# A one-token attention and FFN kernel: weight loads on 128 + 64 partitions, a split last V chunk, late softmax normalisation and a pre-gated FFN row

## The chip, the cores and the metric

The kernel runs on one core of a Trainium2 chip. The metric is device time in microseconds (us), best read as a median of several executions. A profile of one execution is looked at beside it; its span is about 1.8 us shorter than the time. Some numbers are taken from the trace's own records: of every DMA packet it has start, length and size, and of every load it has the sixteen moments at which the load's sixteen shares landed; I take one share for one of the sixteen DMA engines, which the records do not name. PE is the matrix engine, ACT and DVE are the two engines for element-wise work, and SP issues the loads. In this kernel PE's results go to the memory PSUM, and the loaded tensors lie in the memory SBUF on 128 partitions or fewer, each with its own rows. A granted clock of 1.00 is PE's full clock in the profile, 0.50 half of it.

## The reference

A single token `x` (448 values) goes through attention with 16 query heads over 8 cached K/V heads of 65536 keys (head size 256), and through a gated FFN. The two rows are mixed by a sigmoid gate.

```python
def reference(A_x, A_k_cache, A_v_cache, A_wq, A_wo, B_x, B_W_gate, B_W_up, B_W_down, gate_w):
    x = A_x                                            # [1, 1, 448], bf16
    g = sigmoid((x * gate_w).sum(-1, keepdims=True))
    q = (x @ A_wq) as 16 heads of 256
    p = softmax(q @ k.T * 256 ** -0.5)                 # k, v: [8, 65536, 256], each used by two heads
    a = (p @ v) as one row of 4096 @ A_wo
    b = (relu(x @ W_gate) * (x @ W_up)) @ W_down       # F = 1792
    return g * a + (1 - g) * b
```

K and V are 537 MB together. Every byte is used once, so this is a kernel that streams.

## The kernel before

One queue (the SP engine's) issues all loads in a fixed order into a ring of seven slots of 2 MB. A slot is reloaded when PE has consumed what lay in it. PE transposes K groups (ACT moves them from PSUM to SBUF), multiplies them with q, and later multiplies the transposed probabilities with V. The weights share one SBUF region, `wreg`.

The parts that the change touches (cuts marked):

```python
KC = 112                                   # 448 rows of weights = 112 partitions x 4 rows
wq_v = wreg[0:KC, 0:NKC * HQ * DH].rearrange("p (c n) -> p c n", c=NKC)
# ... W_gate and W_up likewise; W_down and A_wo are on 128 partitions

# SP: the stream of loads
sp.dma_start(xT[:, :], ...); sp.dma_start(gwT[:, :], ...)
sp.dma_start(wq_v, A_wq.rearrange("(p c) n -> p c n", c=NKC)).then_inc(s_wq, 16)
for i, (kind, p, c) in enumerate(stream):  # 256 chunks of 2 MB
    # ... wait until the slot is free
    sp.dma_start(ring[:, b], chunk_src(kind, p, c)).then_inc(s_arr[b], 16)
    # after chunk 3: W_gate, W_up, W_down; after chunk 18: A_wo

# PE: PV, 16 matmuls per chunk, in turn on three column tiles (NPV = 3) of one PSUM bank
ins = pe.matmul(ps[32 * ct:32 * ct + 4, PV, :], lhsT=pT_bf[...], rhs=ring[:, b, 2 * k:2 * k + 2, :], ...)

# DVE, at the end of each head: scale the three tiles one after the other
for ct in range(NPV):
    ins = dve.tensor_scalar(o8[32 * ct:32 * ct + 4, p % 2, :], ps[32 * ct:32 * ct + 4, PV, :],
                            rl[32 * ct:32 * ct + 4, p:p + 1], None, ALU.mult)
# PE: OT (sum of the tiles, transposed) -> DVE: copy to oT -> PE: N (times A_wo)
# DVE, at the very end: out = (N - b) * g + b
n = self_inc(dve.tensor_tensor(res_f[R, :], row_ps(), b_sb[R, :], ALU.subtract))
dve.scalar_tensor_tensor(res_b[R, :], res_f[R, :], e_sb[R, 2:3], b_sb[R, :], ALU.mult, ALU.add)
```

## Time and profile before

| What | Before |
|---|---|
| time, median of the 13 runs beside the change's | 1325.9 us |
| span of the profiled execution | 1322.7 us |
| bytes loaded | 549 MB |
| PE / ACT / DVE busy | 73% / 42% / 3% |
| last V chunk has landed | 1312.8 us |
| from there to the end | 9.9 us |

The page of the kernel before cuts the span into 40 slices. `PEclk` is the granted clock of PE in tenths, `DMA` the busy share of the 16 DMA engines in tenths, `GB/s` what they moved.

```profile
PEclk9799988979879988988889889888988889888866
DMA  9999999999999999999999999999999999999994
GB/s 316 336 427 418 420 427 428 428 428 427 427 427 428 428 426 427 428 427 426 428 427 427 427 428 427 427 427 427 428 427 427 427 428 425 429 428 427 428 428 197
```

The DMA engines are busy throughout, and 427 to 428 GB/s is their steady rate. The kernel is bound by its loads. Only the first two slices and the last fall short, so these are where time can be won. The stretch table gives, for each stretch of the kernel before, the busy time of PE, PEld (weight loading), DVE, ACT and POOL, then the granted clock, the DMA share and GB/s.

```profile
2.00:19.00 17.00, 0.20 (x8) 0.23 (x9) 1.43 (x6) 0.01 (x1) 0.00 (x0) 1.00 0.98 261
36.00:53.00 17.00, 8.29 (x82) 5.62 (x80) 0.00 (x0) 7.12 (x14) 0.00 (x0) 0.92 1.01 251
1300.00:1309.00 9.00, 3.75 (x31) 1.09 (x32) 0.00 (x0) 0.00 (x0) 0.00 (x0) 0.64 0.52 224
```

From 2 to 19 us `A_wq` loads, and from 36 to 53 us `W_gate` and `W_up`. The engines are fully busy (shares 0.98 and 1.01) and move 60% of their steady rate. At the end it is different: the busy share is one half, because eight of the sixteen shares have landed or nearly so. The first share of the last chunk landed at 1298.05 us, seven of them by 1299.8, the eighth at 1303.9 and the slowest at 1312.8.

The end of the chain of waits of the kernel before: start, duration, and what it was (engine, tile written, line).

```profile
1281.41 31.39 DMA ring<-in_A_v_cache_dram
1312.84 2.40 PE ps L422 x16
1315.26 0.74 DVE o L609
1316.03 0.75 DVE o L609
1316.81 0.76 DVE o L609
1318.13 1.67 PE ps L474 x4
1319.83 0.64 DVE res_f L636
1320.49 0.69 DVE res_b L638
```

After the last landing all is serial: 16 matmuls of the probabilities with V (PV, L422), three scalings (L609), the four matmuls with `A_wo` (L474), two final operations.

### The profile page before, as it was taken

The numbers are of one execution on the slowest core, as the hardware profiler recorded it, in microseconds if no ns is written. First come the engines' busy times: TensorE is split into PE (matmuls) and PEld (weight loads), VectorE is DVE, ScalarE is ACT, GpSimd is POOL, SyncE is SP. The second block draws the span as 40 slices with busy tenths as digits, with TensorE's granted clock in tenths as the row PEclk, the third lists the DMA queues.
The fourth block names the chain that finished last, engine by engine and source line by source line (L and its number), as shares of the span: only waits on it lengthen the run. The fifth ranks groups of instructions, "written<-read, shape, count | busy, mean of one in ns | idle before, by whom it ended". The sixth has DMA issues, their size and how long they took to land.

```text
span 1322.7 us, 18879 instructions
## 1 busy us (share of the span) xinstructions
PE 959.0 (73%) x8618; PEld 636.2 (48%) x8618; DVE 43.6 (3%) x113; ACT 556.4 (42%) x1066; POOL 0.6 (0%) x6
## 2 busy tenths in 40 slices
PE   3499876768777777777777687776977768767644
PEld 3377554545554455455544454453645445455211
DVE  0000000000000100001000010000100000000101
ACT  2368543435444444434434354442634435434100
POOL 0000000000000000000000000000000000000000
PEclk9799988979879988988889889888988889888866
DMA  9999999999999999999999999999999999999994
GB/s 316 336 427 418 420 427 428 428 428 427 427 427 428 428 426 427 428 427 426 428 427 427 427 428 427 427 427 427 428 427 427 427 428 425 429 428 427 428 428 197
DMA packets 43505, 550.25 MB, mean 416 GB/s; under 512 B 4433, under 2 KB 10322, under 8 KB 10322
## 3 DMA queue, kind: packets, MB, share of 16 engines
q1 hardware_dynamic: 43426, 549.05, 98.8%
q8 instruction: 68, 1.11, 0.3%
q14 instruction: 11, 0.09, 0.0%
HBM read 549.03 MB, written 0.00 MB: 415 GB/s over the span
## 4 chain that ended last, share of the span: by engine, by line
DMA 74%; PE 24%; ACT 1%; DVE 0%; issue 0%; SPq 0%
DMA ring<-in_A_k_cache_dram 64%; PE ps L376 16%; DMA ring<-in_A_v_cache_dram 9%; PE ps L395 4%; PE ps L422 3%; DMA wreg<-in_A_wq_dram 1%; ACT pb L515 1%; PE ps L356 0%; ACT ktb L525 0%; PE ps L493 0%; DVE o L609 0%; PE ps L437 0%; PE ps L474 0%; PE ps L433 0%; PE ps L483 0%
## 5 line engine op out<-in xcount | busy, mean ns | idle before, releaser
L525 ACT COPY ktb<-ps 128x512 f32<-128x512 f32 x1024 | 540.1, 598 | 644.4 <-PE ps L376 643.3
L376 PE MATMUL ps<-ident_f,ring 128*128 128x128 f32 x4096 | 594.4, 306 | 262.0 <-DMA ring<-in_A_k_cache_dram 256.8
L376 PEld LDWEIGHTS ps<-ident_f,ring 128*128 128x128 f32 x4096 | 518.7, 158 | 396.0 <-DMA ring<-in_A_k_cache_dram 307.7
L422 PE MATMUL ps<-ring,pT_all 128*4 128x512 bf16 x2048 | 207.3, 409 | 74.5 <-DMA ring<-in_A_v_cache_dram 72.6
L395 PE MATMUL ps<-ktb,zq 128*32 128x512 bf16 x2048 | 177.7, 424 | 0.0
L422 PEld LDWEIGHTS ps<-ring,pT_all 128*4 128x4 bf16 x2048 | 66.5, 87 | 193.5 <-DMA ring<-in_A_v_cache_dram 108.1
L395 PEld LDWEIGHTS ps<-ktb,zq 128*32 128x32 bf16 x2048 | 31.9, 96 | 49.9 <-ACT ktb L525 48.6
L577 DVE TENSOR_REDUCE mB<-ps 128x1 f32<-128x512 f32 x8 | 5.5, 691 | 649.4 <-PE ps L395 649.4
L609 DVE TENSOR_SCALAR o<-ps,rl 4x512 bf16<-4x512 f32 x24 | 17.8, 743 | 63.5 <-PE ps L422 63.0
L577 DVE TENSOR_REDUCE mA<-ps 128x1 f32<-128x512 f32 x8 | 5.5, 691 | 386.9 <-PE ps L395 386.9
L356 PE MATMUL ps<-xT,wreg 112*128 112x1 bf16 x128 | 3.6, 165 | 18.8 <-DMA wreg<-in_A_wq_dram 18.8
L515 ACT ACTIVATE pb<-ps,negM 128x512 bf16<-128x512 f32 x16 | 10.8, 682 | 7.2 <-DVE negM L593 7.2
L356 PEld LDWEIGHTS ps<-xT,wreg 112*128 112x128 bf16 x128 | 3.5, 104 | 18.8 <-issue 18.8
L474 PE MATMUL ps<-wreg,oT 128*1 128x448 bf16 x32 | 8.1, 379 | 2.0 <-DVE oT L617 2.0
L510 ACT ACTIVATE e_sb<-ps 1x1 f32<-1x1 f32 x1 | 0.2, 163 | 20.8 <-DVE zq L555 20.8
L530 ACT COPY pT_all<-ps 128x512 f32<-128x512 f32 x8 | 4.7, 586 | 9.4 <-PE ps L453 9.4
L453 PE MATMUL ps<-ident_b,pb 128*128 128x128 bf16 x64 | 5.2, 228 | 0.0
L453 PEld LDWEIGHTS ps<-ident_b,pb 128*128 128x128 bf16 x64 | 4.7, 114 | 0.0
L462 PEld LDWEIGHTS ps<-sel_b,o 128*128 128x128 bf16 x32 | 1.3, 98 | 6.9 <-issue 3.5
L442 PEld LDWEIGHTS ps<-rs,wpar_f 128*128 128x128 f32 x16 | 2.6, 203 | 4.0 <-issue 4.0
L437 PEld LDWEIGHTS ps<-ident_f,negR 1*128 1x128 f32 x16 | 2.3, 182 | 3.6 <-issue 3.6
L462 PE MATMUL ps<-sel_b,o 128*128 128x2 bf16 x32 | 2.0, 167 | 2.4 <-DVE o L609 2.4
(45 smaller groups left out, 43.4 us busy)
## 6 DMA issues: line engine op xcount, KB each, us to landing
ring<-in_A_k_cache_dram SPq DMA_DIRECT2D x128, 2048.0 KB, 31.5
ring<-in_A_v_cache_dram SPq DMA_DIRECT2D x128, 2048.0 KB, 29.6
wreg<-in_A_wq_dram SPq DMA_DIRECT2D x1, 3584.0 KB, 17.0
wreg<-in_A_wo_dram SPq DMA_DIRECT2D x1, 3584.0 KB, 31.5
wreg<-in_B_W_gate_dram SPq DMA_DIRECT2D x1, 1568.0 KB, 24.5
wreg<-in_B_W_up_dram SPq DMA_DIRECT2D x1, 1568.0 KB, 30.6
wreg<-in_B_W_down_dram SPq DMA_DIRECT2D x1, 1568.0 KB, 34.1
xT<-in_A_x_dram SPq DMA_DIRECT2D x1, 0.9 KB, 1.8
```

Source lines behind the costliest of these rows:

```text
L356: ins = pe.matmul(ps[:, PX, XC_Q + cq:XC_Q + cq + 1], lhsT=wq_v[:, ic, hq * DH + par:(hq + 1) * DH:2], rhs=xT[:, ic:ic + 1], start=(ic == ...
L376: ins = pe.transpose(ps[:, ts % 3, s * 128:(s + 1) * 128], ring[:, b, j, :].bitcast(F32), ident_f[:, :])
L395: ins = pe.matmul(ps[32 * c:32 * c + 32, bank, :], lhsT=zq[:, p, par, 30 - 2 * u:62 - 2 * u], rhs=kt_bf[:, par:1024:2], start=(u == 0 and ...
L422: ins = pe.matmul(ps[32 * ct:32 * ct + 4, PV, :], lhsT=pT_bf[:, p % 2, col0:col0 + 4], rhs=ring[:, b, 2 * k:2 * k + 2, :], start=(kk == ct ...
L453: ins = pe.transpose(dstv[:, o0:o0 + 128], pb[:, p % 2, bb, s * 128:(s + 1) * 128], ident_b[:, :])
L462: ins = pe.matmul(ps[:, PX, XO + hf * 2:XO + hf * 2 + 2], lhsT=o8[:, p % 2, sp_ * 256 + hf * 128:sp_ * 256 + (hf + 1) * 128], rhs=sel_b[:, ...
L474: ins = pe.matmul(row_ps(), lhsT=oT[:, cc:cc + 1], rhs=wo_sb[:, cc, :], start=(p == 0 and k == 0), stop=(p == HKV - 1 and k == 3), tile_po ...
L515: ins = act.activation(pb[:, p % 2, bb, :], ps[:, sbank(p, bb), :], AF.Exp, bias=negM[:, p:p + 1], scale=1.0, accum_out=rs[:, p, bb:bb + 1])
L525: act.copy(ktb[:, g % NKT, :], ps[:, ts % 3, :]).then_inc(s_ev, 1)
L530: act.copy(pT_all[:, p % 2, :].rearrange("k (bb r s) -> k bb r s", bb=2, r=GPB, s=4), ps[:, ts % 3, :].rearrange("k (bb s r) -> k bb r s", ...
L577: return self_inc(dve.tensor_reduce(dst[:, p:p + 1], ps[:, sbank(p, bb), :], AX.X, ALU.max))
L609: ins = dve.tensor_scalar(o8[32 * ct:32 * ct + 4, p % 2, :], ps[32 * ct:32 * ct + 4, PV, :], rl[32 * ct:32 * ct + 4, p:p + 1], None, ALU.mult)
```

## The change

Its name speaks of the decode tail, but it also changes how the weights are laid out. The core of the diff, with cuts:

```diff
-    KC = 112
-    NKC = D // KC
+    NKA = 3                                  # 384 rows on 128 partitions ...
+    KB = D - 128 * NKA                       # ... and 64 rows on 64 partitions
+    NKC = NKA + 1
-            sp.dma_start(wq_v, A_wq.rearrange("(p c) n -> p c n", c=NKC)).then_inc(s_wq, 16)
+            sp.dma_start(wqA, A_wq[0:128 * NKA, :].rearrange("(p c) n -> p c n", c=NKA)).then_inc(s_wq, 16)
+            sp.dma_start(wqB, A_wq[128 * NKA:D, :]).then_inc(s_wq, 16)
 ...  (W_gate, W_up, x and gate_w are split in the same way)
+    TAIL=((0, 16), (16, 8), (24, 8)),        # the last V chunk as three loads
 ...
+        def npv_of(p):                       # two column tiles in the last head
+            return 2 if (p == HKV - 1 and NPV > 2) else NPV
 ...
-                    ins = dve.tensor_scalar(o8[...], ps[32 * ct:32 * ct + 4, PV, :], rl[...], None, ALU.mult)
+                    ins = dve.tensor_copy(o8[...], ps[32 * ct:32 * ct + 4, PV, :])   # last head: tile 0
+                act.copy(o8[32:36, (HKV - 1) % 2, :], ps[32:36, PV, :])              # last head: tile 1
 ...
-                dve.tensor_copy(oT[...], ps[:, PX, XO:XO + 4]...)
+                dve.tensor_tensor(oT[...], ps[:, PX, XO:XO + 4]..., rlq[...], ALU.mult)   # 1/sum here
 ...
-                dve.tensor_copy(b_sb[R, :], row_ps())
+                dve.tensor_scalar(gb_sb[R, :], row_ps(), e_sb[R, 3:4], None, ALU.mult)    # (1-g)*b, early
-            n = self_inc(dve.tensor_tensor(res_f[R, :], row_ps(), b_sb[R, :], ALU.subtract))
-            dve.scalar_tensor_tensor(res_b[R, :], res_f[R, :], e_sb[R, 2:3], b_sb[R, :], ALU.mult, ALU.add)
+            dve.scalar_tensor_tensor(res_b[R, :], row_ps(), e_sb[R, 2:3], gb_sb[R, :], ALU.mult, ALU.add)
```

The intent: loads without odd partition counts at the start, and after the last byte 4 matmuls instead of 16, one PSUM copy time instead of three, one final operation instead of two.

More of the change, by code (lines that the diff above doesn't have):

```diff
@@ L39, in bass_gated_mix__gqa_block_cached__glu_gated_reglu__decode_kernel @@
     assert DH == 256 and HQ == 2 * HKV
-    KC = 112
-    NKC = D // KC
-    assert NKC * KC == D
+    NKA = 3
+    KB = D - 128 * NKA
+    assert 0 < KB <= 128
+    NKC = NKA + 1
     FC = 128
@@ L76, in bass_gated_mix__gqa_block_cached__glu_gated_reglu__decode_kernel, with geom @@
             vi += 1
-    for c in range(CPH):
+    for c in range(CPH - 1):
         stream.append(("V", HKV - 1, c))
+    sub = {}
+    for (j0, n) in TAIL:
+        item = ("V", HKV - 1, CPH - 1 + len(sub))
+        sub[item] = (CPH - 1, j0, n)
+        stream.append(item)
+    assert sum(n for (_, n) in TAIL) == CS and all(n % 2 == 0 and j0 % 2 == 0 for (j0, n) in TAIL)
     NCHUNK = len(stream)
+    def geom(item):
+        if item in sub:
+            return sub[item]
+        return (item[2], 0, CS)
     def gidx(p, c, gi):
@@ L190, in bass_gated_mix__gqa_block_cached__glu_gated_reglu__decode_kernel @@
         ring = es.enter_context(nc.sbuf_tensor("ring", [128, NB, CS, DH], BF))
-        wreg = es.enter_context(nc.sbuf_tensor("wreg", [128, NKC * F * 2 + NFC * D], BF))
+        WREG = max(NKC * HQ * DH, 2 * NKC * F + NFC * D)
+        wreg = es.enter_context(nc.sbuf_tensor("wreg", [128, WREG], BF))
         ktb = es.enter_context(nc.sbuf_tensor("ktb", [128, NKT, 512], F32))
@@ L202, in bass_gated_mix__gqa_block_cached__glu_gated_reglu__decode_kernel @@
         sel_f = es.enter_context(nc.sbuf_tensor("sel_f", [128, 32], F32))
-        sel_b = es.enter_context(nc.sbuf_tensor("sel_b", [128, 4], BF))
-        xT = es.enter_context(nc.sbuf_tensor("xT", [KC, NKC], BF))
-        gwT = es.enter_context(nc.sbuf_tensor("gwT", [KC, NKC], BF))
+        sel_b = es.enter_context(nc.sbuf_tensor("sel_b", [128, 2, 4], BF))
+        ones_f = es.enter_context(nc.sbuf_tensor("ones_f", [128, 128], F32))
+        rsq = es.enter_context(nc.sbuf_tensor("rsq", [128, HKV, 2], F32))
+        gb_sb = es.enter_context(nc.sbuf_tensor("gb_sb", [RP + 1, D], F32))
+        xT = es.enter_context(nc.sbuf_tensor("xT", [128, NKC], BF))
+        gwT = es.enter_context(nc.sbuf_tensor("gwT", [128, NKC], BF))
         oT = es.enter_context(nc.sbuf_tensor("oT", [128, NQC], BF))
@@ L215, in bass_gated_mix__gqa_block_cached__glu_gated_reglu__decode_kernel @@
         rs2 = es.enter_context(nc.sbuf_tensor("rs2", [128, HKV], F32))
-        rl = es.enter_context(nc.sbuf_tensor("rl", [128, HKV], F32))
+        rlq = es.enter_context(nc.sbuf_tensor("rlq", [128, HKV, 2], F32))
         r_sb = es.enter_context(nc.sbuf_tensor("r_sb", [128, NFC], F32))
         hT = es.enter_context(nc.sbuf_tensor("hT", [128, NFC], BF))
-        b_sb = es.enter_context(nc.sbuf_tensor("b_sb", [RP + 1, D], F32))
         e_sb = es.enter_context(nc.sbuf_tensor("e_sb", [RP + 1, 4], F32))
-        res_f = es.enter_context(nc.sbuf_tensor("res_f", [RP + 1, D], F32))
         res_b = es.enter_context(nc.sbuf_tensor("res_b", [RP + 1, D], BF))
@@ L243, in bass_gated_mix__gqa_block_cached__glu_gated_reglu__decode_kernel, with wsplit, wparts @@
         pT_bf = pT_all[:, :, :].bitcast(BF)
-        wq_v = wreg[0:KC, 0:NKC * HQ * DH].rearrange("p (c n) -> p c n", c=NKC)
-        wg_v = wreg[0:KC, 0:NKC * F].rearrange("p (c n) -> p c n", c=NKC)
-        wu_v = wreg[0:KC, NKC * F:2 * NKC * F].rearrange("p (c n) -> p c n", c=NKC)
+        def wsplit(off, n):
+            a = wreg[:, off:off + NKA * n].rearrange("p (c n) -> p c n", c=NKA)
+            b = wreg[0:KB, off + NKA * n:off + NKC * n]
+            return a, b
+        wqA, wqB = wsplit(0, HQ * DH)
+        wgA, wgB = wsplit(0, F)
+        wuA, wuB = wsplit(NKC * F, F)
         wd_v = wreg[:, 2 * NKC * F:2 * NKC * F + NFC * D].rearrange("p (c n) -> p c n", c=NFC)
-        assert NKC * HQ * DH <= NKC * F * 2 + NFC * D
-        assert NQC * D <= NKC * F * 2 + NFC * D
+        assert NQC * D <= WREG
         wo_sb = wreg[:, 0:NQC * D].rearrange("p (c n) -> p c n", c=NQC)
+        def wparts(A, B, ic, cols):
+            if ic < NKA:
+                return A[:, ic, cols], xT[:, ic:ic + 1]
+            return B[:, cols], xT[0:KB, NKA:NKA + 1]
         def sem(name):
@@ L285, in bass_gated_mix__gqa_block_cached__glu_gated_reglu__decode_kernel @@
         s_on = sem("on")
+        s_on2 = sem("on2")
         s_ot = sem("ot")
@@ L290, in bass_gated_mix__gqa_block_cached__glu_gated_reglu__decode_kernel, with chunk_src @@
         s_out = sem("out")
-        NSETUP = 9
+        NSETUP = 12
         dve_cnt = [0]
-        def chunk_src(kind, p, c):
+        def chunk_src(item):
+            kind, p, _ = item
+            c, j0, n = geom(item)
             cache = A_k_cache if kind == "K" else A_v_cache
             rows = cache[0, p, c * CS * 128:(c + 1) * CS * 128, :]
-            return rows.rearrange("(p j) d -> p j d", p=128)
+            return rows.rearrange("(p j) d -> p j d", p=128)[:, j0:j0 + n, :]
         W1_AFTER = min(3, NCHUNK - 1)
@@ L303, in bass_gated_mix__gqa_block_cached__glu_gated_reglu__decode_kernel @@
         nv = 0
+        vlast = {}
         for (kind, p, c) in stream:
@@ L306, in bass_gated_mix__gqa_block_cached__glu_gated_reglu__decode_kernel @@
                 vchunk_no[(p, c)] = nv
+                vlast[p] = nv
                 nv += 1
@@ L310, in _ @@
         def _(sp):
-            sp.dma_start(xT[:, :], A_x[0, 0, :].rearrange("(p c) -> p c", c=NKC)).then_inc(s_x, 16)
-            sp.dma_start(gwT[:, :], gate_w.rearrange("(p c) -> p c", c=NKC)).then_inc(s_gw, 16)
-            sp.dma_start(wq_v, A_wq.rearrange("(p c) n -> p c n", c=NKC)).then_inc(s_wq, 16)
+            xv = A_x[0, 0, :]
+            sp.dma_start(xT[:, 0:NKA], xv[0:128 * NKA].rearrange("(p c) -> p c", c=NKA)).then_inc(s_x, 16)
+            sp.dma_start(xT[0:KB, NKA:NKC], xv[128 * NKA:D].rearrange("(p c) -> p c", c=1)).then_inc(s_x, 16)
+            sp.dma_start(gwT[:, 0:NKA], gate_w[0:128 * NKA].rearrange("(p c) -> p c", c=NKA)).then_inc(s_gw, 16)
+            sp.dma_start(gwT[0:KB, NKA:NKC], gate_w[128 * NKA:D].rearrange("(p c) -> p c", c=1)).then_inc(s_gw, 16)
+            sp.dma_start(wqA, A_wq[0:128 * NKA, :].rearrange("(p c) n -> p c n", c=NKA)).then_inc(s_wq, 16)
+            sp.dma_start(wqB, A_wq[128 * NKA:D, :]).then_inc(s_wq, 16)
             for i, (kind, p, c) in enumerate(stream):
@@ L321, in _ @@
                         sp.wait_ge(s_pvc, vchunk_no[(p0, c0)] + 1)
-                sp.dma_start(ring[:, b], chunk_src(kind, p, c)).then_inc(s_arr[b], 16)
+                n_ = geom((kind, p, c))[2]
+                sp.dma_start(ring[:, b, 0:n_], chunk_src((kind, p, c))).then_inc(s_arr[b], 16)
                 if i == W1_AFTER:
                     sp.wait_ge(s_qpe, 1)
-                    sp.dma_start(wg_v, B_W_gate.rearrange("(p c) n -> p c n", c=NKC)).then_inc(s_w1, 16)
-                    sp.dma_start(wu_v, B_W_up.rearrange("(p c) n -> p c n", c=NKC)).then_inc(s_w1, 16)
+                    sp.dma_start(wgA, B_W_gate[0:128 * NKA, :].rearrange("(p c) n -> p c n", c=NKA)).then_inc(s_w1, 16)
+                    sp.dma_start(wgB, B_W_gate[128 * NKA:D, :]).then_inc(s_w1, 16)
+                    sp.dma_start(wuA, B_W_up[0:128 * NKA, :].rearrange("(p c) n -> p c n", c=NKA)).then_inc(s_w1, 16)
+                    sp.dma_start(wuB, B_W_up[128 * NKA:D, :]).then_inc(s_w1, 16)
                     sp.dma_start(wd_v, B_W_down.rearrange("(c p) n -> p c n", p=FC)).then_inc(s_w1, 16)
@@ L349, in _ @@
             pe.wait_ge(s_setup, NSETUP)
-            pe.wait_ge(s_x, 16)
-            pe.wait_ge(s_wq, 16)
+            pe.wait_ge(s_x, 32)
+            pe.wait_ge(s_wq, 32)
             for hq in range(HQ):
@@ L355, in _ @@
                     for ic in range(NKC):
-                        ins = pe.matmul(ps[:, PX, XC_Q + cq:XC_Q + cq + 1],
-                                        lhsT=wq_v[:, ic, hq * DH + par:(hq + 1) * DH:2],
-                                        rhs=xT[:, ic:ic + 1], start=(ic == 0), stop=(ic == NKC - 1))
-            pe.wait_ge(s_gw, 16)
+                        w_, x_ = wparts(wqA, wqB, ic, slice(hq * DH + par, (hq + 1) * DH, 2))
+                        ins = pe.matmul(ps[:, PX, XC_Q + cq:XC_Q + cq + 1], lhsT=w_, rhs=x_,
+                                        start=(ic == 0), stop=(ic == NKC - 1))
+            pe.wait_ge(s_gw, 32)
             for ic in range(NKC):
-                ins = pe.matmul(ps[RP:RP + 1, PX, XC_Z:XC_Z + 1], lhsT=xT[:, ic:ic + 1], rhs=gwT[:, ic:ic + 1],
+                if ic < NKA:
+                    l_, r_ = xT[:, ic:ic + 1], gwT[:, ic:ic + 1]
+                else:
+                    l_, r_ = xT[0:KB, NKA:NKC], gwT[0:KB, NKA:NKC]
+                ins = pe.matmul(ps[RP:RP + 1, PX, XC_Z:XC_Z + 1], lhsT=l_, rhs=r_,
                                 start=(ic == 0), stop=(ic == NKC - 1), tile_position=(0, RP))
@@ L410, in do_PV @@
                         pe.wait_ge(s_ffn4, 1)
-                for k in range(CS // 2):
-                    kk = c * (CS // 2) + k
-                    ct = kk % NPV
+                cg, j0, n_ = geom(("V", p, c))
+                npv = npv_of(p)
+                for k in range(n_ // 2):
+                    kk = (cg * CS + j0) // 2 + k
+                    ct = kk % npv
                     sidx = 2 * kk
@@ L420, in do_PV @@
                     col0 = ((bb * GPB + r_) * 4 + s) * 2
-                    last_kk = ((NPAIR - 1 - ct) // NPV) * NPV + ct
+                    last_kk = ((NPAIR - 1 - ct) // npv) * npv + ct
                     ins = pe.matmul(ps[32 * ct:32 * ct + 4, PV, :], lhsT=pT_bf[:, p % 2, col0:col0 + 4],
@@ L441, in do_aux @@
                     pe.wait_ge(s_r2, p + 1)
-                    pe.matmul(ps[:, PX, XC_L:XC_L + 1], lhsT=wpar_f[:, :], rhs=rs2[:, p:p + 1],
+                    pe.matmul(ps[:, PX, XC_L:XC_L + 2], lhsT=ones_f[:, :], rhs=rsq[:, p, :],
                               start=True, stop=True).then_inc(s_j, 1)
@@ L457, in do_aux @@
                     pe.wait_ge(s_on, p + 1)
+                    if p == HKV - 1 and npv_of(p) == 2 and NPV > 2:
+                        pe.wait_ge(s_on2, 1)
                     if p + 1 < HKV:
                         pe.wait_ge(s_l, p + 2)
+                    selv = sel_b[:, 1 if npv_of(p) == 2 and NPV != 2 else 0, :]
                     for hf in range(2):
@@ L463, in do_aux @@
                                             lhsT=o8[:, p % 2, sp_ * 256 + hf * 128:sp_ * 256 + (hf + 1) * 128],
-                                            rhs=sel_b[:, sp_ * 2:sp_ * 2 + 2], start=(sp_ == 0), stop=(sp_ == 1))
+                                            rhs=selv[:, sp_ * 2:sp_ * 2 + 2], start=(sp_ == 0), stop=(sp_ == 1))
                     ins.then_inc(s_ot, 1)
@@ L478, in do_aux @@
                 elif name == "FFN1":
-                    pe.wait_ge(s_w1, 48)
+                    pe.wait_ge(s_w1, 80)
                     pe.wait_ge(s_e, 1)
-                    for fc in range(NFC):
-                        for ic in range(NKC):
-                            pe.matmul(ps[:, PX, XC_G + fc:XC_G + fc + 1], lhsT=wg_v[:, ic, fc * 128:(fc + 1) * 128],
-                                      rhs=xT[:, ic:ic + 1], start=(ic == 0), stop=(ic == NKC - 1))
-                    for fc in range(NFC):
-                        for ic in range(NKC):
-                            ins = pe.matmul(ps[:, PX, XC_U + fc:XC_U + fc + 1], lhsT=wu_v[:, ic, fc * 128:(fc + 1) * 128],
-                                            rhs=xT[:, ic:ic + 1], start=(ic == 0), stop=(ic == NKC - 1))
+                    for (A_, B_, xc) in ((wgA, wgB, XC_G), (wuA, wuB, XC_U)):
+                        for fc in range(NFC):
+                            for ic in range(NKC):
+                                w_, x_ = wparts(A_, B_, ic, slice(fc * 128, (fc + 1) * 128))
+                                ins = pe.matmul(ps[:, PX, xc + fc:xc + fc + 1], lhsT=w_, rhs=x_,
+                                                start=(ic == 0), stop=(ic == NKC - 1))
                     ins.then_inc(s_ffn1, 1)
@@ L528, in _ @@
                     if p >= 2:
-                        act.wait_ge(s_pvc, vchunk_no[(p - 2, CPH - 1)] + 1)
+                        act.wait_ge(s_pvc, vlast[p - 2] + 1)
                     act.copy(pT_all[:, p % 2, :].rearrange("k (bb r s) -> k bb r s", bb=2, r=GPB, s=4),
                              ps[:, ts % 3, :].rearrange("k (bb s r) -> k bb r s", bb=2, r=GPB, s=4)).then_inc(s_ev, 1)
+            if npv_of(HKV - 1) == 2 and NPV > 2:
+                act.wait_ge(s_pvc, vlast[HKV - 1] + 1)
+                act.copy(o8[32:36, (HKV - 1) % 2, :], ps[32:36, PV, :]).then_inc(s_on2, 1)
         @block.vector
@@ L552, in _ @@
             dve.wait_ge(s_setup, 8)
-            dve.tensor_copy(sel_b[:, :], sel_f[:, 0:4]).then_inc(s_setup, 1)
+            dve.tensor_copy(sel_b[:, 0, :], sel_f[:, 0:4]).then_inc(s_setup, 1)
+            dve.wait_ge(s_setup, 9)
+            dve.tensor_reduce(sel_f[:, :], ident_f[:, 0:64].rearrange("m (ct r) -> m r ct", ct=2),
+                              AX.X, ALU.add).then_inc(s_setup, 1)
+            dve.wait_ge(s_setup, 10)
+            dve.tensor_copy(sel_b[:, 1, :], sel_f[:, 0:4]).then_inc(s_setup, 1)
+            dve.memset(ones_f[:, :], 1.0).then_inc(s_setup, 1)
             dve.wait_ge(s_qpe, 1)
@@ L569, in ffn_end @@
             def ffn_end():
+                dve.wait_ge(s_dve, n_g)
+                n = self_inc(dve.tensor_scalar(e_sb[R, 3:4], e_sb[R, 2:3], -1.0, 1.0, ALU.mult, ALU.add))
+                dve.wait_ge(s_dve, n)
                 dve.wait_ge(s_ffn3, 1)
-                dve.tensor_copy(b_sb[R, :], row_ps()).then_inc(s_ffn4, 1)
+                dve.tensor_scalar(gb_sb[R, :], row_ps(), e_sb[R, 3:4], None, ALU.mult).then_inc(s_ffn4, 1)
             def red(p, bb):
@@ L596, in rsum @@
                 dve.wait_ge(s_pt, p + 1)
-                dve.tensor_tensor(rs2[:, p:p + 1], rs[:, p, 0:1], rs[:, p, 1:2], ALU.add).then_inc(s_r2, 1)
+                n = self_inc(dve.tensor_tensor(rs2[:, p:p + 1], rs[:, p, 0:1], rs[:, p, 1:2], ALU.add))
+                dve.wait_ge(s_dve, n)
+                dve.tensor_scalar(rsq[:, p, :], wpar_f[:, 0:2], rs2[:, p:p + 1], None, ALU.mult).then_inc(s_r2, 1)
             def chain4(p):
                 dve.wait_ge(s_j, p + 1)
-                dve.reciprocal(rl[:, p:p + 1], ps[:, PX, XC_L:XC_L + 1]).then_inc(s_l, 1)
+                dve.reciprocal(rlq[:, p, :], ps[:, PX, XC_L:XC_L + 2]).then_inc(s_l, 1)
             def norm(p):
-                dve.wait_ge(s_pvc, vchunk_no[(p, CPH - 1)] + 1)
-                dve.wait_ge(s_l, p + 1)
-                for ct in range(NPV):
-                    if ct == NPV - 1 and NPV > 1:
+                dve.wait_ge(s_pvc, vlast[p] + 1)
+                npv = npv_of(p)
+                tiles = list(range(npv))
+                if p == HKV - 1 and npv == 2:
+                    tiles = [0]
+                for k_, ct in enumerate(tiles):
+                    if k_ == len(tiles) - 1 and len(tiles) > 1:
                         dve.wait_ge(s_dve, dve_cnt[0])
-                    ins = dve.tensor_scalar(o8[32 * ct:32 * ct + 4, p % 2, :], ps[32 * ct:32 * ct + 4, PV, :],
-                                            rl[32 * ct:32 * ct + 4, p:p + 1], None, ALU.mult)
-                    if ct < NPV - 1:
+                    ins = dve.tensor_copy(o8[32 * ct:32 * ct + 4, p % 2, :], ps[32 * ct:32 * ct + 4, PV, :])
+                    if k_ < len(tiles) - 1:
                         self_inc(ins)
@@ L616, in otcopy @@
                 dve.wait_ge(s_ot, p + 1)
-                dve.tensor_copy(oT[:, 4 * p:4 * p + 4].rearrange("d (q hf) -> d hf q", hf=2),
-                                ps[:, PX, XO:XO + 4].rearrange("d (hf q) -> d hf q", q=2)).then_inc(s_m, 1)
+                dve.wait_ge(s_l, p + 1)
+                dve.tensor_tensor(oT[:, 4 * p:4 * p + 4].rearrange("d (q hf) -> d hf q", hf=2),
+                                  ps[:, PX, XO:XO + 4].rearrange("d (hf q) -> d hf q", q=2),
+                                  rlq[:, p:p + 1, :].broadcast_to([128, 2, 2]), ALU.mult).then_inc(s_m, 1)
             ffn_mid()
@@ L635, in _ @@
             dve.wait_ge(s_n, HKV)
-            n = self_inc(dve.tensor_tensor(res_f[R, :], row_ps(), b_sb[R, :], ALU.subtract))
-            dve.wait_ge(s_dve, max(n, n_g))
-            dve.scalar_tensor_tensor(res_b[R, :], res_f[R, :], e_sb[R, 2:3], b_sb[R, :], ALU.mult, ALU.add).then_inc(s_fin, 1)
+            dve.scalar_tensor_tensor(res_b[R, :], row_ps(), e_sb[R, 2:3], gb_sb[R, :], ALU.mult, ALU.add).then_inc(s_fin, 1)
 _INS = ['A_x', 'A_k_cache', 'A_v_cache', 'A_wq', 'A_wo', 'B_x', 'B_W_gate', 'B_W_up', 'B_W_down', 'gate_w']
```

## The prediction

> **What bounds it now.** The span is 1322.7 us; DMA carries 549 MB. The page's slices show 427-428 GB/s and full DMA share from about 66 us to 1290 us, with PE 73% and ACT 42% busy: the ring's load stream is the limit. Three places fall short (stretch table):
> - 2 to 19 us: 261 GB/s. A_wq (3.67 MB, on 112 partitions) takes about 15.8 us; at 428 GB/s it would take 8.6.
> - 36 to 53 us: 251 GB/s, W_gate and W_up on 112 partitions. By the trace's landing events each 1.6 MB takes 6.5 us; at full rate 3.75.
> - 1298 to 1313 us: about 220 GB/s. The sixteen shares of the last V chunk land from 1298.1 to 1312.8: eight DMA engines lag by 12 to 15 us. The lag grows steadily over the run; the suspect is 68 instruction-fetch packets of 16 KB, about 1 us each, not the weights, after which the spread is only about 2 us.
>
> After the last landing comes a serial tail of 9.9 us (timeline): 16 PV matmuls 2.4, three normalisations on DVE 2.3, OT and its copy 0.6, N 1.65, DVE subtract 0.63, combine 0.69, output DMA 1.5.
>
> **What the change does.**
> 1. Weights: 384 rows on 128 partitions, 64 rows on 64. [...] Estimate: A_wq = 3.15 MB at 428 (7.35 us)[...]; gate and up each 3.2[...]. Saved: 6.0 us on A_wq, 2 x 2.2 on gate and up; four small loads instead of two delay A_wq by 0.85. Net 9.5 us, all on the critical path, since every later load queues behind. This, not the tail, is most of the gain.
> 2. Last chunk in 16, 8 and 8 rows: 4 matmuls after the last landing instead of 16. Two column tiles take two rounds of 0.43 us plus a backlog, 1.1 us instead of 2.4. Saves 1.3. The DMA itself ends no sooner.
> 3. Normalisation moved to the 128x4 OT copy: one DVE copy (0.75) beside one ACT copy (0.6) instead of three DVE ops in a row. Saves 1.5.
> 4. Gated FFN precomputed: one final DVE op instead of two. Saves 0.65.
> 5. Set-up ops, two-column row sum, its DVE multiply: off the path, PE has slack. NPV=2 costs at most 3.4 us per chunk against 4.9 of arrival. The engine lag remains, as the number of PE instructions does.
>
> **Sum:** 9.5 + 3.5 = 13 us, about 1%.
> **Predicted:** 1312.7 us, range 1308.5 to 1317.5; faster by over 2%: 0.03; within 2%: 0.96; slower: 0.01.
>
> **Signs.** Right if A_wq has landed by about 13.5 us and the first K transposes start near 18.5 (23.6 before); the 36-53 dip shrinks by 4 to 5 us; the last V lands near 1303; from there to the end takes about 6.3 us; the V shares still spread by 12 to 15 us.
>
> **What would make it wrong.** [...] The lag of eight engines could shift; removing it wholly would be worth about 7 us more. [...] The two readers of one PSUM bank could run one after the other (0.6 us lost).

One term of the estimate is cut for each of the three weights, so the savings of 6.0 and 2 x 2.2 us can't be worked out again from what is left; with the cut terms the sum came to 9.5 + 3.5 = 13 us. What the trace of the kernel before did show is that loads on 112 partitions were slow: their 32 KB packets took 2.08 us at the median, where the ring's 16 KB packets took 0.61 and so twice the bytes would take 1.22. The other figures are estimates from that trace too: its first loads were issued 0.44 and 0.45 us apart (0.85 for two more), a round of PV matmuls took 0.43 us, and the last chunks arrived 4.9 us apart.

## The result, and the profile after

The changed kernel takes 1314.13 us (median of 7; before, on the same chip, 1325.9). The ratio is 0.991, 95% interval 0.990 to 0.992. The change is 0.9% faster, and the predicted 1312.7 us is 1.4 us off.

The slices after:

```profile
DMA  8999999999999999999999999999999999999996
GB/s 343 385 427 411 428 427 427 426 427 428 426 429 426 427 427 426 428 427 427 426 427 428 427 427 427 426 428 427 427 426 428 427 428 425 428 425 428 426 427 254
```

The same stretches of the changed kernel (the last one moved with the end):

```profile
2.00:19.00 17.00, 2.25 (x32) 2.06 (x32) 1.95 (x9) 0.01 (x1) 0.00 (x0) 1.00 0.90 317
36.00:53.00 17.00, 12.27 (x120) 8.93 (x118) 0.00 (x0) 10.29 (x21) 0.00 (x0) 0.99 1.05 349
1294.00:1303.00 9.00, 6.42 (x30) 1.50 (x28) 0.00 (x0) 0.00 (x0) 0.00 (x0) 0.50 0.52 220
```

Of what the two dips lacked to 427 GB/s, about a third (261 to 317) and a bit over half (251 to 349) is made up, the steady rate is the same 427, and the half-empty end is as it was. The end of its chain:

```profile
1284.66 22.52 DMA ring<-in_A_v_cache_dram
1307.22 0.62 PE ps L467 x4
1307.86 0.69 DVE o L672
1309.11 0.93 PE ps L522 x4
1310.06 0.69 DVE res_b L700
```

The span fell by 10.4 us. The last landing moved from 1312.8 to 1307.2, which is 5.6 us, and the time from there to the end fell from 9.93 to 5.13, which is 4.8 us. The medians differ by more, 11.8 us, because the profiled execution of the kernel before took 1324.5 us, 1.4 less than its median; this last part has no profile that explains it.

Where the 5.6 us come from can be read off the packet records. For each size I took the time of all packets above that of the same bytes at the ring packets' steady rate (16 KB in 0.61 us), and divided by 16 engines:

```
excess DMA time per engine, first 66 us      before     after
A_wq    32 KB packets, 112 partitions         5.55        -
        24 KB packets, 128 partitions           -        0.83
         8 KB packets,  64 partitions           -        0.99
W_gate, W_up  14.3 KB, 112 partitions         5.77        -
              10.8 KB, 128 partitions           -        1.26
               3.6 KB,  64 partitions           -        0.70
sum                                          11.32       3.78
first data of A_wq at                         2.69       4.16 us
```

Weights saved 7.54 us of engine time and the stream started 1.47 us later: 6.07 us net. The engine that finishes first ended 5.96 us sooner (1298.05 to 1292.09), the last one 5.61. The gain of the first 60 us thus reappears 1250 us later, undiminished within half a us. In this stream, which is always busy, next to nothing was absorbed on the way.

### The profile page after: what moved, and what is told of

It reads as the page before. It is cut to its first block, busy times and chain, and to the rows that moved or that the text cites. A ratio compares the mean times of both kernels' runs of the same rounds, so it can differ in the third digit from the quotient of the medians.

```text
span 1312.3 us, 18898 instructions
## 1 busy us (share of the span) xinstructions
PE 977.4 (74%) x8618; PEld 648.1 (49%) x8618; DVE 42.6 (3%) x122; ACT 556.8 (42%) x1067; POOL 0.6 (0%) x6
## 3 DMA queue, kind: packets, MB, share of 16 engines
q8 instruction: 68, 1.11, 0.3%
## 4 chain that ended last, share of the span: by engine, by line
DMA 73%; PE 25%; ACT 1%; SPq 0%; issue 0%; DVE 0%
DMA ring<-in_A_k_cache_dram 65%; PE ps L419 16%; DMA ring<-in_A_v_cache_dram 6%; PE ps L438 4%; PE ps L467 3%; DMA wreg<-in_A_wq_dram 1%; ACT pb L561 1%; PE ps L396 1%; PE ps L533 1%; PE ps L539 0%; ACT ktb L571 0%; PE ps L482 0%; PE ps L478 0%; PE ps L522 0%; DVE negM L651 0%
## 5 line engine op out<-in xcount | busy, mean ns | idle before, releaser
L467 PE MATMUL ps<-ring,pT_all 128*4 128x512 bf16 x2048 | 218.1, 410 | 72.8 <-DMA ring<-in_A_v_cache_dram 72.8
L467 PEld LDWEIGHTS ps<-ring,pT_all 128*4 128x4 bf16 x2048 | 70.1, 87 | 199.6 <-DMA ring<-in_A_v_cache_dram 106.5
L396 PE MATMUL ps<-xT,wreg 128*128 128x1 bf16 (+1 forms) x128 | 9.2, 174 | 16.8 <-DMA wreg<-in_A_wq_dram 16.8
L396 PEld LDWEIGHTS ps<-xT,wreg 128*128 128x128 bf16 (+1 forms) x128 | 8.3, 106 | 17.6 <-issue 16.7
L672 DVE CAST o<-ps 4x512 bf16<-4x512 f32 x22 | 14.9, 677 | 61.0 <-PE ps L467 60.5
L522 PE MATMUL ps<-wreg,oT 128*1 128x448 bf16 x32 | 7.3, 351 | 2.0 <-DVE oT L680 2.0
L533 PE MATMUL ps<-xT,wreg 128*128 128x1 bf16 x112 | 7.8, 172 | 0.0
L533 PEld LDWEIGHTS ps<-xT,wreg 128*128 128x128 bf16 x112 | 6.9, 101 | 1.3 <-issue 0.4
```

Of the source, the lines that this page charges most:

```text
L396: ins = pe.matmul(ps[:, PX, XC_Q + cq:XC_Q + cq + 1], lhsT=w_, rhs=x_, start=(ic == 0), stop=(ic == NKC - 1))
L467: ins = pe.matmul(ps[32 * ct:32 * ct + 4, PV, :], lhsT=pT_bf[:, p % 2, col0:col0 + 4], rhs=ring[:, b, 2 * k:2 * k + 2, :], start=(kk == ct ...
L522: ins = pe.matmul(row_ps(), lhsT=oT[:, cc:cc + 1], rhs=wo_sb[:, cc, :], start=(p == 0 and k == 0), stop=(p == HKV - 1 and k == 3), tile_po ...
L533: ins = pe.matmul(ps[:, PX, xc + fc:xc + fc + 1], lhsT=w_, rhs=x_, start=(ic == 0), stop=(ic == NKC - 1))
L672: ins = dve.tensor_copy(o8[32 * ct:32 * ct + 4, p % 2, :], ps[32 * ct:32 * ct + 4, PV, :])
```

## The experiments

Twelve kernels ran. All gave correct results. Each is set against runs of the kernel before on its own chip (medians there 1325.27 to 1325.63 us).

### The two halves alone

The first kernel is the one before with the new weight layout and nothing else; the second is the changed one with the old weights put back.

```diff
 e1:  before + the wqA/wqB, wgA/wgB, wuA/wuB loads and their matmuls; tail as before
 e2:  after  - those;  112 partitions again; tail as changed
```

> The kernel before with the new weight layout alone, tail untouched. Theory (packet accounting of the two traces): 7.5 us less DMA time per engine in the head, 1.5 us later start, so 6 us of gain: 1319.5 to 1320.5 us, with the last V landing near 1307 and a tail of 9.9 us as before. Rival (the projection's matmuls, 9.2 us in the changed kernel against 3.6 before, hold back the K work and eat into it): gain under 3 us, above 1323.

> The changed kernel with the 112-partition weights put back: split last chunk, two column tiles, late normalisation, gated FFN. Theory: landings stay as in the kernel before (last V near 1313), tail 5.1 us instead of 9.9, so 1320.5 to 1321.5 us. If the two parts are additive, this gain and that of the weights-only kernel sum to the 11.8 us of the whole change within 1 us. Rival (the tail's gain came partly from work that the earlier head moved): under 3 us of gain.

Measured: weights only 1318.45 us (ratio 0.9943, 0.9929 to 0.9956), tail only 1320.15 us (0.9965, 0.9949 to 0.9981). The gains are 0.57% and 0.35%, in sum 0.92%, against 0.9% for the whole change. Within the intervals they are additive, and the weights, which the change's name doesn't mention, are the larger half. The last V landing was at 1306.3 us with the new weights and at 1313.2 us with the old ones; the tails were 10.3 and 5.1 us. Both kernels were a little faster than expected (1319.5 and 1320.5 were the lower ends), by less than the spread of the runs. The rival of the first is out: its gain is 7 us, not under 3.

### The split, and the three PSUM copies

```diff
 e3:  -    TAIL=((0, 16), (16, 8), (24, 8)),
      +    TAIL=((0, 32),),
 e4:  -            return 2 if (p == HKV - 1 and NPV > 2) else NPV
      +            return NPV
```

> The changed kernel with the last V chunk in one piece (still two column tiles). Theory: 16 matmuls after the last landing in eight rounds of two at 0.43 us, 3.4 to 3.6 us, instead of 0.6: 2.9 us slower than the changed kernel, 1317.0 us; the last landing itself unmoved within 0.5 us. Rival (the split saves only what the prediction said, 1.3 us): 1315.4 us.

> The changed kernel with three column tiles in the last head too, so that three DVE copies of PSUM follow one another and ACT helps with none. Theory: three copies of 0.68 us instead of one beside ACT, 1.3 to 1.4 us more, less about 0.2 us in the matmuls: 1315.2 to 1315.5 us. Rival (the copies overlap with something else, or two tiles cost as much PE time as they save): within 0.4 us of the changed kernel.

Measured: without the split 1316.02 us (ratio 0.993), with three tiles 1316.08 (0.9929), against the changed kernel's 0.991. Both are slower than it by 1.9 us in the medians and by 2.5 to 2.7 us by the ratios (it ran on another chip). In the profiles the tails are 6.42 and 7.73 us, against 5.13.

For the split my expectation of 2.9 us missed: the tail is 1.3 us longer, as the rival had it. I had taken the 16 matmuls at half clock. They ran at full clock and took 1.91 us:

```profile
1308.40 1.91 PE ps L467 x16
```

For the three tiles the tail is 2.6 us longer, twice my 1.3. The chain of the three-tiles kernel shows why:

```profile
1306.58 1.02 PE ps L467 x3
1307.63 0.68 DVE o L672
1308.34 0.69 DVE o L672
1309.06 0.70 DVE o L672
1310.33 1.67 PE ps L522 x4
1312.02 0.69 DVE res_b L700
```

The two more copies cost 1.4 us as expected. But the last V matmuls took 1.02 us instead of 0.62, and the product with `A_wo` (L522) 1.67 instead of 0.93. The granted clock, third from the end in the stretch table, differs. The changed kernel:

```profile
1307.00:1309.00 2.00, 0.85 (x8) 0.26 (x8) 0.79 (x2) 0.58 (x1) 0.00 (x0) 1.00 0.00 0
1309.00:1310.20 1.20, 0.92 (x4) 0.25 (x4) 0.19 (x2) 0.00 (x0) 0.00 (x0) 1.00 0.00 0
```

The three-tiles kernel:

```profile
1306.00:1307.70 1.70, 1.01 (x4) 0.09 (x4) 0.07 (x1) 0.00 (x0) 0.00 (x0) 0.64 0.00 0
1307.70:1309.80 2.10, 0.00 (x0) 0.00 (x0) 1.98 (x3) 0.00 (x0) 0.00 (x0) 0.50 0.00 0
1309.80:1312.10 2.30, 1.92 (x8) 0.53 (x8) 0.24 (x2) 0.00 (x0) 0.00 (x0) 0.50 0.00 0
```

The kernel before was at 0.50 in this stretch as well:

```profile
1318.00:1320.00 2.00, 1.65 (x4) 0.34 (x4) 0.25 (x2) 0.00 (x0) 0.00 (x0) 0.50 0.00 0
```

What sets the granted clock, the traces do not say. My guess was how busy PE had been just before: 5.64 of the 7 us before 1307 in the changed kernel, 2.86 of the 6 before 1306 with three tiles. If so, PE kept busy should run `A_wo` in 0.93 us with three tiles too. Test: six matmuls of unused result after each of the last V pieces.

```diff
 e12 (on e4):
                 ins.then_inc(s_pvc, 1)
+                if p == HKV - 1 and c >= CPH - 3:
+                    for _ in range(6):
+                        pe.matmul(ps[:, 0, :], lhsT=ident_b[:, :], rhs=pb[:, p % 2, 0, :], start=True, stop=True)
```

> The three-tiles kernel with six idle-time matmuls (result unused) after each of the last V pieces, to keep PE busy. Theory (in the three-tiles tail PE idled 2.2 us and ran at half clock, so its last matmuls took 1.0 and N 1.65 us, where the changed kernel at full clock took 0.6 and 0.92): granted clock near 1.0 up to N, tail 6.6 us instead of 7.7, about 1 us faster than the three-tiles kernel. Rival (N's time has to do with what precedes it, not the clock): N stays at 1.65 us, or the extra matmuls delay the last ones by more than they give.

```profile
1307.21 0.97 PE ps L474 x4
1309.17 0.68 DVE o L676
1309.88 0.69 DVE o L676
1310.60 0.70 DVE o L676
1311.85 0.93 PE ps L526 x4
1312.81 0.69 DVE res_b L704
```

The clock was 1.00 from 1306 us on, the last V matmuls took 0.59 us, and the product with `A_wo` (now L526) 0.93 us: in this execution, with PE busy for all 6 us before 1306, the clock was up over the whole tail. The speed-up did not come. The fillers stood in the queue ahead of the last V pieces, so that the last matmuls began at 1308.5 although their data had landed at 1306.1. The tail grew to 9.0 us and the time to 1316.93 (ratio 0.9935, three tiles 0.9929). My expected 1 us of gain was wrong.

The records of the clock show more than the averages of the stretches. In all fourteen profiles the granted clock changes only after 3.41 us or a multiple of it, and near the end a stretch at full clock is mostly 6.83 us long. In the changed kernel the last one ran from 1305.33 to 1312.16, over the whole tail. In the three-tiles kernel it ran from 1299.66 to 1306.49 and ended 0.1 us before the last V matmuls, so the longer copies, which come after them, did not take the clock away. In the kernel before it ran from 1306.39 to 1313.22 and ended 0.4 us after the last landing. Where it ends also differs between executions: among the ten profiles with two tiles the product with `A_wo` took 0.93 us in eight, but 1.11 in the second profile of the changed kernel and 1.39 in that of the weights-first kernel below, where the stretch ended within it. In the three profiles with three tiles and no fillers it took 1.66 or 1.67. So two tiles go with a faster tail, but by how much is partly a matter of where the stretch falls. That they do it by keeping PE busier with the last chunks (5.64 us of the 7 before 1307, against 2.86 of the 6 before 1306 with three tiles) is argued; the fillers ran before and during the copies and do not single it out.

### The start of the stream and the 64-partition loads

```diff
 e5:  A_wq's two loads are issued before the four loads of x and gate_w
 e6:  e5, and
      -            b = wreg[0:KB, off + NKA * n:off + NKC * n]
      +            b = wreg[:, off + NKA * n:off + NKA * n + n // 2]
      -            sp.dma_start(wqB, A_wq[128 * NKA:D, :])
      +            sp.dma_start(wqB, A_wq[128 * NKA:D, :].rearrange("r (h n) -> (r h) n", h=2))
         partition 2r+h has half h of row r; it is multiplied with a column that has x[r] there and 0 in
         the other half's partitions
```

> The changed kernel with A_wq issued before the four small x and gate_w loads. Theory (the later start of the stream, 4.16 us against 2.69, is paid in full at the end): first data near 1.8 us, 2.3 us gained, about 1311.8 us, ratio to the kernel before near 0.9893. Rival (the start is absorbed somewhere in the 1300 us of streaming): within 0.5 us of the changed kernel's 1314.1 us.

> As weights_first, and the last 64 rows of A_wq, W_gate and W_up spread over 128 partitions as half rows, with x masked to match, so that no load has fewer than 128 partitions. Theory [...]: packets of the small loads at nominal time, 1.7 us less DMA time per engine, about 1310 us; and the projection's 128 matmuls, 9.2 us in the changed kernel, go back to about 3.6 us if the mix of 128-row and 64-row operands is what slowed them. Rival (it is the size of the packets that costs, not the partitions): no gain over weights_first, since the packets are half as long.

Weights first: 1312.07 us (ratio 0.9904, 0.9889 to 0.9919). Its four runs lie between 1310.7 and 1314.2, so the 2.3 us are neither shown nor ruled out. In the profile, of the slowest of its four runs, data began at 1.76 us, 2.4 us sooner, but the first K chunk had landed only 0.7 us sooner: the 64-partition packets took 667 ns at the mean (552 in the changed kernel), and the summed excess of the weights rose from 3.78 to 4.84 us. So in that execution most of the earlier start was gone by the first K chunk, with the loads still uneven. Its tail was also 0.45 us longer, by the clock in the product with `A_wo`.

Even rows: 1308.92 us (ratio 0.988), four runs within 0.5 us. The packets of the last rows of `A_wq` took 159 ns where the steady rate gives 153, while the 64-partition ones had taken 552 where it gives 305. That is 1.04 times the steady-rate time on 128 partitions and 1.8 times on 64. The even-rows packets are half as long, so the rival (packet size) would have had them no better. In the stretches, the two dips are gone:

```profile
13.00:19.00 6.00, 3.85 (x133) 3.76 (x134) 0.50 (x3) 0.16 (x1) 0.00 (x0) 1.00 1.00 426
36.00:53.00 17.00, 5.62 (x49) 4.24 (x48) 0.00 (x0) 4.22 (x9) 0.00 (x0) 0.71 1.04 418
```

A side effect of the change that costs nothing shows here as well. The projection's 128 matmuls, by group (busy us, mean ns of one), before and changed:

```profile
L356 PE MATMUL ps<-xT,wreg 112*128 112x1 bf16 x128 | 3.6, 165 | 18.8 <-DMA wreg<-in_A_wq_dram 18.8
```

```profile
L396 PE MATMUL ps<-xT,wreg 128*128 128x1 bf16 (+1 forms) x128 | 9.2, 174 | 16.8 <-DMA wreg<-in_A_wq_dram 16.8
```

With 128-row and 64-row operands in turn the group takes 9.2 us. With even rows, where all have 128, it takes 3.5 again, in two groups that run in turn:

```profile
L407 PE MATMUL ps<-xT,wreg 128*128 128x1 bf16 x96 | 3.5, 165 | 13.4 <-DMA xm<-in_A_x_dram 13.4
L407 PE MATMUL ps<-xm,wreg 128*128 128x1 bf16 x32 | 3.5, 165 | 0.0
```

It is off the path, since the ring goes on filling meanwhile (422 GB/s from 19 to 36 us in the changed kernel).

### The lag of eight engines

In every kernel here the sixteen shares of the last load land some 15 us apart. Means of the eight later shares minus means of the eight earlier ones, with the number of 16 KB instruction-fetch packets so far:

```
kernel          chunk:     40           100           200          last
before          lag   2.5 (14)      5.4 (30)      9.7 (55)     11.9 (68)
changed         lag   2.3 (14)      4.8 (30)      9.5 (55)     11.7 (68)
more fetches    lag   1.3 (18)      4.3 (37)     10.2 (69)     12.7 (84)
```

The third line is this experiment:

```diff
 e7 (on after):
                 ring_wait(ts)
+                for _ in range(2):
+                    pe.matmul(ps[0:1, ts % 3, 0:1], lhsT=ident_b[:, 0:1], rhs=ident_b[:, 0:1], start=True, stop=True)
```

> The changed kernel with two tiny extra matmuls per transpose group, overwritten at once: 4096 PE instructions more, so 16 more instruction fetches (84 for 68), same data traffic, same results. Theory (the lag of eight DMA engines comes from the fetches, 1.5 us of lag for each on its engine): spread of the last V landing grows from 15.1 to about 18.5 us, the fast engines end where they did, the kernel is 3.4 us slower. Rival (the lag comes from the data transfers themselves): spread stays near 15, time within 1 us as PE has slack.

The 1.5 us per fetch was an estimate; the changed kernel's 11.7 us of lag in 68 fetches would give 8 x 11.7 / 68 = 1.38 if eight engines take them in turn. The run had 84 fetches as planned and took 1323.75 us (ratio 0.9989), 10 us slower than the changed kernel, not 3.4. The spread at the end was 14.5 us, not 18.5. By its own expectation it failed, for a reason that I should have seen: in the first head, where only K is streamed, PE had no room for the extra matmuls.

```profile
99.00:200.00 101.00, 100.91 (x995) 66.38 (x994) 2.75 (x9) 68.33 (x120) 0.00 (x0) 1.00 0.96 382
200.00:1290.00 1090.00, 931.60 (x8782) 557.40 (x8782) 34.04 (x91) 505.64 (x879) 0.00 (x0) 0.94 1.01 427
```

PE was busy for all of 99 to 200 us, the stream fell to 382 GB/s, and the engines that were ahead gave up part of their lead (1.3 us at chunk 40, against 2.3 in the changed kernel). From 200 us on the stream was whole, and there the test is good. From chunk 40 to the last, the changed kernel's lag grew by 9.4 us in 54 fetches and this one's by 11.4 us in 66. With eight engines that take the fetches in turn, that is 8 x 9.4 / 54 = 1.39 and 8 x 11.4 / 66 = 1.38 us per fetch on its engine, in the same 1052 us. Over the same chunks and the same time the lag grew with the fetches, which supports the prediction's suspect; a fetch packet itself takes 1.07 us at the mean. It is one execution with more fetches. Of the other twelve profiles with 68 fetches, ten show 9.4 or 9.5 us of growth like the changed kernel, but the two attempts below, whose queue was disturbed, 8.4 (1.24 us per fetch). That the fetches go in turn to eight engines and to no others is an assumption of mine and not shown, since the packets' records do not name the engine.

By my estimate (half of the 11.7 us of lag, or of the 15.1 of spread) the lag is worth some 6 to 7 us to whoever can spread it. Two attempts to put a load on eight of the sixteen engines alone, by copies of 8 partitions:

```diff
 e8 (on after):  A_wo in 16 copies of 8 partitions
-                    sp.dma_start(wo_sb, A_wo.rearrange("(c p) n -> p c n", p=128)).then_inc(s_wo, 16)
+                    for b0 in range(0, 128, 32):
+                        for a0 in range(4):
+                            q = slice(b0 + a0, b0 + 32, 4)
+                            sp.dma_start(wo_sb[q], wo_d[q]).then_inc(s_wo, 16)
 e10 (on e9):    W_gate and W_up as 64 partitions x 7 rows, in the same kind of copies
```

> The changed kernel with A_wo (3.67 MB) loaded by 16 copies of 8 partitions each instead of one of 128[...]. If these are the eight that do not lag, they end about 10 us later and the laggards 10 us sooner: spread under 8 us and the kernel 4 to 5 us faster. If they are the laggards, the spread grows to above 30 us and the kernel is about 10 us slower. Third case (the engines are not bound to the work like that): nothing moves.

> As long_rows, but W_gate and W_up on 64 partitions only, in copies of 8 partitions, which go to 8 of the 16 DMA engines (as seen with A_wo). If those are the engines that do not lag, the laggards are spared 7.5 us of work: spread of the last landing from 14.6 to about 8 us or less, 1300 us. If they are the laggards, spread to 22 us, 1314 us. If the queue holds back the other eight meanwhile, as it did with A_wo, both halves end later, about 1314 us with the spread unchanged.

That a copy of 8 partitions runs on eight engines was an assumption. What was measured: while `A_wo` loaded this way the engines' busy share was 0.54 to 0.55, as with about half of them at work. So the rest did not go on with the ring's next chunks, they idled. All sixteen ended about 12 us later, the spread stayed at 15.7 us, and the time was 1325.21 us (ratio 1.0003). My two first cases fell, and it doesn't tell which eight engines lag.

With `W_gate` and `W_up`, whose packets are 25 KB and not 896 bytes, the others did go on: after them eight engines were ahead by 14.7 us. A fetch fell on one of these: that at 65.1 us moved a share of the leading group from an expected 66.2 to 67.7 us. So, as far as this fetch tells, the load lay on the right engines. Still the time was 1315.02 us (ratio 0.9919), slower than its base of 1308.72. The stretches show where the lead went:

```profile
66.00:80.00 14.00, 14.00 (x179) 11.38 (x177) 0.00 (x0) 8.22 (x16) 0.00 (x0) 1.00 1.01 427
80.00:100.00 20.00, 20.00 (x218) 16.06 (x216) 1.88 (x5) 7.65 (x15) 0.00 (x0) 0.74 0.75 315
```

A chunk counts as landed when its slowest share has (in the kernel before, the last chunk's slowest at 1312.79, its matmuls from 1312.84). PE waited 17 us for the first chunk after the weights, then had the FFN's 196 small matmuls (10.6 us) and was busy throughout; the seven slots were full, the leading engines had nothing to load, and at chunk 19 the lag was 2.3 us again. This came too early in the stream; a place where PE has slack was not tried.

### A better version, and the changed kernel once more

```diff
 e9 (on e6):  f and d indices mapped so that a partition's rows of W_down and A_wo lie together
-    B_W_down.rearrange("(c p) n -> p c n", p=FC)
+    B_W_down.rearrange("(h p j) n -> p h (j n)", h=2, j=7)          # runs of 6272 bytes for 896
-    A_wo.rearrange("(c p) n -> p c n", p=128)
+    A_wo.rearrange("(g p t) n -> p g (t n)", p=128, t=2)            # runs of 1792 bytes
     with W_gate/W_up columns and o8 columns taken in the matching stride
```

> As even_rows, and W_down and A_wo mapped so that a partition's rows lie together: runs of 6272 and 1792 bytes instead of 896. Theory (each 896-byte packet takes 41 ns where 33 would be nominal, a fixed 7.6 ns): 0.85 + 0.97 us less DMA time per engine, 1307 us. Rival (that time is hidden): no gain over even_rows, 1308.9 us.

> The changed kernel once more, to stand on the same chip as the others of this call: ratio to the kernel before 0.991 as on record, within 0.15%.

Of the figures of the first, 41 ns is the median of the 896-byte packets in the traces, 33 ns is 896 bytes at the ring packets' rate, and the 7.6 ns between them were taken to be the same for longer packets, which is an assumption.

Long rows: 1308.72 us, ratio 0.9871 (0.9856 to 0.9887). The changed kernel: 1313.89 us, ratio 0.9912 (0.9896 to 0.9927). So this version is 5.2 us faster than the changed kernel by the medians and 17 us faster than the one before. Of the 1.8 us expected from the longer rows over even rows, the last landing showed 0.5 us (1302.4 to 1301.9) and the medians 0.2 us, from different chips; that part is not shown.

## Why the prediction was right or wrong

The total was right: 1312.7 predicted, 1314.1 measured, inside the range. But two terms of the sum were mis-sized, in opposite directions, so that it came this close is partly luck.

- **What bounds the kernel.** Right. The steady rate stayed at 427 and the gain of the head reached the end undiminished (5.6 of 6.1 us).
- **Weights, "Net 9.5 us".** That the new loads save most was right, the size wrong: 6.07 us. "Saved: 6.0 us on A_wq" measured 3.73 (5.55 less 0.83 and 0.99). I had set about 15.8 us, roughly the time from the first data (2.69) to the last landing (18.66), against a pure transfer time for the new loads, the cut term included. Its 112 packets, seven for each of 16 engines, at 2.01 us are 14.1 us; the rest is latency and spread, which the new loads pay too: from first data to last landing they took 12.5. Nor had I given the 128-partition loads any excess (0.83). "2 x 2.2 on gate and up" measured 3.81 in sum (5.77 less 1.96). The delay of 0.85 was 1.47. Why the old loads were slow, no trace shows. That they were (32 KB packets 2014 ns at the mean, where the steady rate gives 1220), and that on 128 partitions most of that was gone (24 KB packets 1019 ns, where it gives 915), is what the runs show. The sign "A_wq landed by 13.5" failed (16.6), as did "first K transposes near 18.5": they began at 26.1, since the projection took 9.2 us, which I did not foresee and which cost nothing.
- **The split, "Saves 1.3".** The mechanism was right, the size too small: the chain's last matmuls fell from 2.40 to 0.62 us, 1.78 less. The experiment without the split had a tail 1.3 us longer, but that the number is the same is luck: it compares 16 with 4 matmuls at full clock, where the prediction had a slower clock in mind for what was left (1.1 us).
- **Late normalisation, "Saves 1.5".** Right: three serial DVE operations of 2.3 us in sum became one of 0.69 beside ACT: both copies out of the one PSUM bank began at 1307.86, and ACT's took 0.58. This and the next point are read from the chains; no run took either alone.
- **One final operation, "Saves 0.65".** Right: 0.64 is gone.
- **Missed: the clock.** The tail was predicted at 6.3 us and was 5.13. The product with A_wo took 0.93 us instead of 1.67 and the last V matmuls 0.62 instead of the 1.1 predicted. The granted clock was 1.00 there and 0.50 before; the three-tiles kernel with fillers, at 1.00 as well, had the same 0.93. The second profile of the changed kernel had 1.11, so part of this is the execution's luck.
- **The engine lag remains.** Right: 15.1 us of spread against 14.7. What it comes from was only suspected; counted per fetch (1.39 and 1.38 us) it holds in the two kernels compared.

So the head was overestimated by 3.4 us and the tail underestimated by 1.3; another 0.5 of the head's gain was lost by the last landing. Between the two profiles that leaves 10.4 us of the 13 predicted. The medians, which differ by 11.8, look kinder to it because the profiled execution of the kernel before was one of its fast ones.

## What to carry to other kernels

In a kernel whose loads never pause, look first at the rates of its odd loads and at the start of its stream: here a microsecond lost there was paid at the end, 1250 us later, nearly in full. Cost a load by the durations of its packets and not by the time from issue to landing, since latency and spread are part of the latter: `A_wq` took 15.97 us from first data to last landing, of which its packets, at seven for each engine, account for 14.1. In a serial tail, read the granted clock before costing the matmuls: the same four took 0.93 us at full clock and 1.67 at half, and which of the two they get can change from one execution to the next.
